# The cast of the output weight to its high part, from ScalarE to VectorE, for weight sets 2 to 11

## The chip, the cores and the metric

The kernel runs on one core of a Trainium2 chip. A core has TensorE (PE, matrix products; its weight loads are shown as PEld), VectorE (DVE), ScalarE (ACT), GpSimd (POOL) and SyncE (SP, which issues the transfers). Each works through its own list of instructions in order and waits for the others by semaphores. The metric is the time of one execution on the device in microseconds (us); before the change it is 969.11 us, the median of 3 runs (968.31 to 970.41).

## The reference, cut to what matters

An attention stage gives x (2304 tokens, 512 wide). Two feed-forward stages follow it:

```
g = x @ w_gate;  val = x @ w_val          # 512 -> 1536
y = (g * sigmoid(g) * val) @ w_out        # 1536 -> 512
h = y @ w2_in                             # 512 -> 2048
out = (max(h, 0) + alpha * min(h, 0)) @ w2_out
```

The inputs q, k, v and all weights are float32 in the reference; the kernel is given the weights as 64-bit floats, which is why a weight element arrives as two 32-bit words and has to be put together on the chip.

## The kernel before, in words

**The first feed-forward stage.** The 2304 tokens are cut into 8 blocks of 288 (HB). The hidden width of 1536 is cut into 12 tiles of 128. Tile j needs weight set j: g (gate), v (value) and o (output), each held as a high part and a low part, so that three products of fp32r stand for one exact product (mm3, L500 to L502: hi by hi, hi by lo, lo by hi). For block and tile PE runs m_g (12 products into g), m_v (12 into v) and, one tile later, m_y (12 into y), 133 ns each at full clock. Between them DVE makes u from g (L544, after a tanh on ACT, L543) and from u and v (L551), ACT casts u to its high part ph (L558) and POOL subtracts to get the low part pl (L559).

**The weights are prepared in the first block only.** For set j the function prep1_ calls w_split for g, v and o in this order, one tile ahead of use. w_split is a chain over three engines: ACT reads the high words with scaling (L129) and the top bytes of the low words (L137); DVE merges the two in place (L139); ACT casts the merged tile st to the high part w[:, 0] (L142); POOL subtracts to get the low part w[:, 1] (L143). For the sets 10 and 11 a shorter buffer is used and DVE merges in two steps, L131 and L132, without L137. st_tile counts its calls in stc[0]: after the o of set j the count is 3(j + 1).

**What else runs in the first block.** The attention of the units from 8 on is prepared beside it: transposes, sums and softmax steps on DVE (L302 to L482), subtractions and sums on POOL (L347, L348, L396, L433, L487), transfers of kn, qn and vd on SP. From the second block on the weights lie ready and only the block's own work and the attention units remain.

**The order.** In this part the order of each engine's list is not written by hand: a scheduler places the instructions by its own estimate of when each can run. So an edit of one instruction moves others on all engines. The names st_1435 and so on below are the merge buffers; st_1340, st_1435, st_1500 belong to the o of the sets 7, 8 and 9, and plain st is the buffer of the sets 10 and 11.

Of the kernel before, what the change touches and what calls it, by code (L numbers as in the profile page):

```python
# [23 lines left out]
def attn_moe_moe2_kernel(  # L24
# [13 lines left out]
    nc = tc.nc  # L38
# [44 lines left out]
    def f32(t):  # L83
        return t.bitcast(F32)
# [26 lines left out]
    stc = [0, None]  # L111

    def top_byte(t):
        return t.rearrange("p f t -> p (f t)").bitcast(U8).rearrange("p (f b) -> p f b", b=8)[:, :, 3]

    def st_tile():
        c = stc[0]
        stc[0] += 1
        if c >= 3 * NEARLY:
            return stp[0].tile([128, 512], F32, tag="st", name="st", bufs=stn[0]), None  # L120
        t = wp.tile([128, 2, 512], F32, tag=st_slots[c % len(st_slots)], name="st2")
        return t[:, 0], t[:, 1]

    def w_split(slot, eng):
        t = raw.pop(slot)
        st, sk = st_tile()
        sti = st.bitcast(I32)
        hw, lw = t[:, :, 1], t[:, :, 0]
        nc.scalar.activation(out=st, in_=hw.bitcast(F32), func=AF.Prelu, scale=2.0 ** -112, alpha=-2.0 ** 32)  # L129
        if sk is None:  # L130
            nc.vector.tensor_scalar(out=sti, in0=sti, scalar1=3, scalar2=None, op0=ALU.logical_shift_left)  # L131
            nc.vector.scalar_tensor_tensor(out=sti, in0=lw, scalar=29, in1=sti,  # L132
                                           op0=ALU.logical_shift_right, op1=ALU.bitwise_or)
        else:

            ski = sk.bitcast(I32)
            nc.scalar.activation(out=ski, in_=top_byte(t), func=AF.Copy,  # L137
                                 scale=1.0 / 32, bias=-31.0 / 64)
            nc.vector.scalar_tensor_tensor(out=sti, in0=sti, scalar=3, in1=ski,  # L139
                                           op0=ALU.logical_shift_left, op1=ALU.bitwise_or)  # L140
        w = W[slot] = wp.tile([128, 2, 512], F32R, tag=slot, name="w")
        nc.scalar.copy(out=w[:, 0], in_=st)  # L142
        eng.tensor_sub(w[:, 1], st, f32(w[:, 0]))  # L143


# [385 lines left out]
    def prep1_(j):  # L531
        for kind in "gvo":
            w_split(f"{kind}{j}", nc.vector if kind in ("", "o", "go", "gvo")[K["lo1"]] else nc.gpsimd)
# [1028 lines left out]
```

## Time and profile before

| what | us |
|---|---|
| median of 3 runs | 969.11 |
| the profiled execution, its own time | 969.31 |
| its span from the first to the last instruction | 967.5 |
| PE busy in the span | 929.8 (96%) |
| DVE busy | 613.2 (63%) |
| ACT busy | 422.7 (44%) |
| POOL busy | 374.2 (39%) |

The shares are means over very different stages. The kernel is full on PE from 135 us on; the change lies in the stretch from 59 to 133 us, where the weights are prepared, and has to be read there.

### The profile page before, as it was taken

To read this page: it belongs to the slowest core of one execution; us is meant where nothing else is said; L and a number is where in the kernel's file an instruction comes from. 1 tells how busy PE (TensorE), PEld (TensorE's weight loads), DVE (VectorE), ACT (ScalarE), POOL (GpSimd) and SP (SyncE) were. 2 spreads that over 40 slices of the span, in tenths; PEclk is the share of its full clock that TensorE was granted. 3 is DMA by queue.
4 is the path that set the end of the run, shared out by engine and by line. 5 is a ranking of instruction groups with operands and counts; after the bars stand their busy time and mean duration, and the time that the engine had idled before them with its cause. 6 is when DMAs were issued, how large, how long until landed. Compare 5 with 4: busy or idle time off the path is not lost.

```text
span 967.5 us, 21670 instructions
## 1 busy us (share of the span) xinstructions
PE 929.8 (96%) x8648; PEld 891.9 (92%) x8648; DVE 613.2 (63%) x1193; ACT 422.7 (44%) x965; POOL 374.2 (39%) x492
## 2 busy tenths in 40 slices
PE   5589889999999999999999998999999999999998
PEld 4479789999999999999999998999999988999998
DVE  5887774546454554535442365777777998777675
ACT  4598732222222132222322356564435774544443
POOL 6389873234422244222222278956251920000000
PEclk9789999999999999999999999999999999999999
DMA  7899641223211141111101346234426882444331
GB/s 190 247 336 373 170 113 34 37 64 59 48 46 24 35 91 34 32 44 22 48 9 53 100 138 212 102 122 149 171 99 231 282 279 87 146 164 150 110 109 44
DMA packets 162091, 116.29 MB, mean 120 GB/s; under 512 B 98889, under 2 KB 143177, under 8 KB 161225
## 3 DMA queue, kind: packets, MB, share of 16 engines
q1 hardware_dynamic: 161927, 114.92, 39.0%
q8 instruction: 67, 1.10, 0.5%
q14 instruction: 33, 0.27, 0.1%
q10 hardware_dynamic: 64, 0.01, 0.0%
HBM read 86.58 MB, written 34.60 MB: 125 GB/s over the span
## 4 chain that ended last, share of the span: by engine, by line
PE 84%; DMA 4%; DVE 3%; POOL 3%; issue 2%; ACT 2%; SPq 1%; DVEq 0%; POOLq 0%; ACTq 0%
PE y L500 5%; PE v L501 5%; PE v L500 5%; PE g L500 4%; PE y L502 4%; PE v L502 4%; PE g L501 4%; PE y L501 4%; PE g L502 4%; PE y L1010 3%; PE y L1011 3%; PE y L1012 3%; PE c L1010 3%; PE c L1011 3%; PE c L1012 3%; PE y L1211 3%
## 5 line engine op out<-in xcount | busy, mean ns | idle before, releaser
L544 DVE SCALAR_TENSOR_TENSOR u<-u,g 128x288 f32<-128x288 f32 x90 | 40.7, 452 | 141.9 <-ACT u L543 141.7
L500 PE MATMUL g<-xh,w 128*128 128x288 f32 x360 | 108.2, 301 | 10.5 <-DVE u L544 4.7
L500 PE MATMUL v<-xh,w 128*128 128x288 f32 x360 | 109.5, 304 | 0.0
L501 PE MATMUL v<-xl,w 128*128 128x288 f32 x360 | 108.9, 302 | 0.0
L502 PE MATMUL g<-xh,w 128*128 128x288 f32 x360 | 107.3, 298 | 0.8 <-POOL w L143 0.8
L502 PE MATMUL v<-xh,w 128*128 128x288 f32 x360 | 107.2, 298 | 0.3 <-POOL w L143 0.3
L501 PE MATMUL g<-xl,w 128*128 128x288 f32 x360 | 107.3, 298 | 0.0
L501 PE MATMUL y<-pl,w 128*128 128x288 f32 x336 | 99.4, 298 | 0.2 <-POOL pl L559 0.2
L502 PE MATMUL y<-ph,w 128*128 128x288 f32 x336 | 99.0, 297 | 0.0
L500 PE MATMUL y<-ph,w 128*128 128x288 f32 x336 | 97.8, 302 | 0.0
L559 POOL TENSOR_TENSOR pl<-u,ph 128x288 fp32r<-128x288 f32 x84 | 70.7, 841 | 57.0 <-ACT ph L558 56.7
L1160 DVE TENSOR_TENSOR hs<-hr,hs 128x512 fp32r<-128x512 f32 x98 | 65.0, 689 | 38.2 <-ACT hs L1154 36.6
L543 ACT ACTIVATE u<-g 128x288 f32<-128x288 f32 x90 | 36.9, 410 | 115.4 <-PE g L502 109.3
L500 PEld LDWEIGHTS g<-xh,w 128*128 128x128 f32 x360 | 68.5, 190 | 12.4 <-DVE u L544 5.4
L558 ACT CAST ph<-u 128x288 fp32r<-128x288 f32 x84 | 36.3, 432 | 89.7 <-DVE u L551 89.7
L501 PEld LDWEIGHTS v<-xl,w 128*128 128x128 f32 x360 | 69.0, 192 | 1.7
L500 PEld LDWEIGHTS v<-xh,w 128*128 128x128 f32 x360 | 68.9, 191 | 1.0 <-DVE u L551 0.5
L502 PEld LDWEIGHTS g<-xh,w 128*128 128x128 f32 x360 | 68.8, 191 | 1.0 <-POOL w L143 1.0
L502 PEld LDWEIGHTS v<-xh,w 128*128 128x128 f32 x360 | 69.0, 192 | 0.5 <-POOL w L143 0.5
L501 PEld LDWEIGHTS g<-xl,w 128*128 128x128 f32 x360 | 68.6, 191 | 0.0
L1154 ACT CAST hs<-hr 128x512 fp32r<-128x512 f32 x98 | 56.9, 622 | 20.6 <-DVE hr L1167 18.8
L500 PEld LDWEIGHTS y<-ph,w 128*128 128x128 f32 x336 | 61.8, 188 | 4.4 <-issue 4.4
(293 smaller groups left out, 2958.7 us busy)
## 6 DMA issues: line engine op xcount, KB each, us to landing
hbuf<-t SPq DMA_DIRECT2D x64, 288.0 KB
hr<-hbuf SPq DMA_DIRECT2D x36, 512.0 KB
raw<-in_moe_w_out_dram SPq DMA_DIRECT2D x28, 512.0 KB
raw<-in_moe_w_in_dram SPq DMA_DIRECT2D x16, 512.0 KB
raw<-in_moe_w_gate_dram SPq DMA_DIRECT2D x12, 512.0 KB
raw<-in_moe_w_val_dram SPq DMA_DIRECT2D x12, 512.0 KB
vw<-vwin SPq DMA_DIRECT2D x48, 96.0 KB
sy<-y SPq DMA_DIRECT2D x8, 576.0 KB
```

Of the source, the lines that this page charges most:

```text
L500: nc.tensor.matmul(o, lhi, rhi, start=first, stop=False)
L501: nc.tensor.matmul(o, lhi, rlo, start=False, stop=False)
L502: nc.tensor.matmul(o, llo, rhi, start=False, stop=last)
L543: nc.scalar.activation(out=u, in_=G[:, :HB], func=AF.Tanh, scale=0.5)
L544: nc.vector.scalar_tensor_tensor(out=u, in0=u, scalar=1.0, in1=G[:, :HB], op0=ALU.add, op1=ALU.mult)
L558: nc.scalar.copy(out=ph, in_=u)
L559: nc.gpsimd.tensor_sub(pl, u, f32(ph))
L1010: nc.tensor.matmul(o, whi[:, ks], yhi[k], start=first, stop=False, skip_group_check=True)
L1011: nc.tensor.matmul(o, whi[:, ks], ylo[k], start=False, stop=False, skip_group_check=True)
L1012: nc.tensor.matmul(o, wlo[:, ks], yhi[k], start=False, stop=k == 1, skip_group_check=True)
L1154: nc.scalar.copy(out=t[:, 0], in_=R[b][SRC[m]])
L1160: vec[0].tensor_sub(t[:, 1], R[b][SRC[m]], f32(t[:, 0]))
```

## The change

In w_split the cast of the merged tile to the high part is given to DVE for the slots whose name begins with o, from the count 7 on, that is for the o of the sets 2 to 11 (10 casts of 128x512). The casts of g and v, and of o of the sets 0 and 1, stay on ACT.

```
         w = W[slot] = wp.tile([128, 2, 512], F32R, tag=slot, name="w")
-        nc.scalar.copy(out=w[:, 0], in_=st)
+        if slot[0] in "o" and stc[0] > 6:
+            nc.vector.tensor_copy(w[:, 0], st)
+        else:
+            nc.scalar.copy(out=w[:, 0], in_=st)
         eng.tensor_sub(w[:, 1], st, f32(w[:, 0]))
```

Lines behind it move down by 3 (L544 becomes L547, L302 becomes L305, and so on).

The first place is DVE's list where the o of the sets 8 and 9 are merged (106 to 116 us in the trace), before:

```order
L139 SCALAR_TENSOR_TENSOR st_1493<-st_1493 128x512
L302 STREAM_TRANSPOSE kT<-kn 128x576
L303 STREAM_TRANSPOSE qT<-qn 128x288
L139 SCALAR_TENSOR_TENSOR st_1435<-st_1435 128x512
L327 TENSOR_REDUCE kd<-kT 128x144
L334 TENSOR_REDUCE qd<-qT 128x72
L139 SCALAR_TENSOR_TENSOR st_1486<-st_1486 128x512
L544 SCALAR_TENSOR_TENSOR u<-u,g 128x288
L131 TENSOR_SCALAR st<-st 128x512
L551 SCALAR_TENSOR_TENSOR u<-u,v 128x288
```

The same place in DVE's list of the changed kernel:

```order
L139 SCALAR_TENSOR_TENSOR st_1435<-st_1435 128x512
L143 CAST w<-st_1435 128x512
L305 STREAM_TRANSPOSE kT<-kn 128x576
L139 SCALAR_TENSOR_TENSOR st_1493<-st_1493 128x512
L306 STREAM_TRANSPOSE qT<-qn 128x288
L330 TENSOR_REDUCE kd<-kT 128x144
L139 SCALAR_TENSOR_TENSOR st_1486<-st_1486 128x512
L337 TENSOR_REDUCE qd<-qT 128x72
L547 SCALAR_TENSOR_TENSOR u<-u,g 128x288
L139 SCALAR_TENSOR_TENSOR st_1500<-st_1500 128x512
L554 SCALAR_TENSOR_TENSOR u<-u,v 128x288
```

The cast of o8 now stands ahead of the transposes and of both u of the tile, and the merge of o9 (st_1500), which stood five rows behind the second u, has moved in front of it.

The second place is the end of the preparation in DVE's list, the merges of the sets 10 and 11 (119 to 132 us), before:

```order
L551 SCALAR_TENSOR_TENSOR u<-u,v 128x288
L426 RECIPROCAL sr_81<-sr_81 128x8
L131 TENSOR_SCALAR st<-st 128x512
L439 TENSOR_TENSOR sm<-sm,sr_81 72x2x144
L131 TENSOR_SCALAR st<-st 128x512
L132 SCALAR_TENSOR_TENSOR st<-raw,st 128x512
L444 STREAM_TRANSPOSE bd_80<-sm 32x6x32 x4
L302 STREAM_TRANSPOSE kT<-kn 128x576
L132 SCALAR_TENSOR_TENSOR st<-raw,st 128x512
L544 SCALAR_TENSOR_TENSOR u<-u,g 128x288
```

And in the changed kernel:

```order
L554 SCALAR_TENSOR_TENSOR u<-u,v 128x288
L131 TENSOR_SCALAR st<-st 128x512
L428 TENSOR_SCALAR sr_81<-sr_81 128x8
L132 SCALAR_TENSOR_TENSOR st<-raw,st 128x512
L429 RECIPROCAL sr_81<-sr_81 128x8
L131 TENSOR_SCALAR st<-st 128x512
L143 CAST w<-st 128x512
L442 TENSOR_TENSOR sm<-sm,sr_81 72x2x144
L132 SCALAR_TENSOR_TENSOR st<-raw,st 128x512
L547 SCALAR_TENSOR_TENSOR u<-u,g 128x288
```

The cast of o10 stands in front of the merge of the next set and of the u that PE needs next; the four transposes L444 have moved behind that u.

## Rows read from the trace of the kernel before

**Rows 1.** Stretches: start:end, length, busy time and instructions of each engine, clock, DMA.

```profile
core 0: us, PE busy (x) PEld busy (x) DVE busy (x) ACT busy (x) POOL busy (x), PEclk, DMA share, GB/s
60.00:98.00 38.00, 35.75 (x336) 34.08 (x335) 29.30 (x50) 32.44 (x74) 33.39 (x30) 0.94 1.02 365
98.34:101.75 3.41, 3.41 (x15) 3.22 (x14) 1.52 (x3) 3.41 (x7) 2.28 (x2) 0.50 0.41 67
110.00:135.00 25.00, 19.41 (x179) 17.20 (x179) 23.19 (x47) 13.73 (x28) 21.24 (x23) 1.00 0.62 141
135.00:250.00 115.00, 115.00 (x1229) 110.12 (x1233) 60.51 (x158) 29.98 (x80) 43.02 (x78) 1.00 0.26 56
250.00:968.00 718.00, 711.62 (x6241) 690.99 (x6240) 448.82 (x822) 299.77 (x662) 230.82 (x275) 1.00 0.34 107
```

**Rows 2.** Waits of PE from 60 to 300 us: total, times, longest.

```profile
PE g L500 <- DVE u L544: 3.3, 2, 2.3
PE g L500 <- ACT w L142: 1.6, 1, 1.6
PE g L500 <- DVE st L131: 1.1, 1, 1.1
PE g L502 <- POOL w L143: 0.8, 1, 0.8
PE att L374 <- DVE qd L334: 0.6, 1, 0.6
PE v L502 <- POOL w L143: 0.3, 1, 0.3
PE y L501 <- POOL pl L559: 0.2, 1, 0.2
```

**Rows 3.** DVE in order of time, the only idle marks from 111 to 134 us.

```profile
111.47 0.69 DVE L139 SCALAR_TENSOR_TENSOR st<-st 128x512 int32<-128x512 int32 x1 [0.86 <-ACT st L137]
...
133.16 0.46 DVE L551 SCALAR_TENSOR_TENSOR u<-u,v 128x288 f32<-128x288 f32 x1 [0.78 <-PE v L502]
```

**Rows 4.** Groups by line: busy us, mean ns, idle before; then shortest/median/longest ns.

```profile
L131 DVE TENSOR_SCALAR st<-st 128x512 int32<-128x512 int32 x6 | 4.5, 750 | 0.0
L131 DVE TENSOR_SCALAR st<-st x6: 404/418/1524, 94.4 to 129.2; 128x512 int32<-128x512 int32 x6
L139 DVE SCALAR_TENSOR_TENSOR st<-st x30: 636/768/1686, 37.2 to 115.3; 128x512 int32<-128x512 int32 x30
L142 ACT CAST w<-st x36: 601/620/636, 40.8 to 132.1; 128x512 fp32r<-128x512 f32 x36
L143 POOL TENSOR_TENSOR w<-st,w x36: 1267/1288/2076, 41.5 to 132.8; 128x512 fp32r<-128x512 f32 x36
L559 POOL TENSOR_TENSOR pl<-u,ph 128x288 fp32r<-128x288 f32 x84 | 70.7, 841 | 57.0 <-ACT ph L558 56.7
```

**Rows 5.** DVE, then POOL, in order of time, 94 to 98 us.

```profile
94.36 1.52 DVE L131 TENSOR_SCALAR st<-st 128x512 int32<-128x512 int32 x1
95.92 1.63 DVE L132 SCALAR_TENSOR_TENSOR st<-raw,st 128x512 int32<-128x512 int32 x1
97.47 0.44 DVE L544 SCALAR_TENSOR_TENSOR u<-u,g 128x288 f32<-128x288 f32 x1
...
94.08 2.92 POOL L143 TENSOR_TENSOR w<-st,w 128x512 fp32r<-128x512 f32 x2 [0.20 <-ACT w L142]
```

**Rows 6.** DVE, then POOL, in order of time, 120 to 123 us.

```profile
120.96 0.41 DVE L131 TENSOR_SCALAR st<-st 128x512 int32<-128x512 int32 x1
121.29 0.67 DVE L132 SCALAR_TENSOR_TENSOR st<-raw,st 128x512 int32<-128x512 int32 x1
...
120.68 1.96 POOL L559 TENSOR_TENSOR pl<-u,ph 128x288 fp32r<-128x288 f32 x1
```

**Rows 7.** All engines' waits from 60 to 140 us: total, times, longest.

```profile
POOL w L143 <- ACT w L142: 7.7, 10, 1.7
ACT st L129 <- DMA raw<-in_moe_w_out_dram: 0.9, 1, 0.9
```

## The prediction, as it was put on record

> **What bounds the kernel now.** I read the stretches first. From 135 us on PE is busy without a gap (115.00 of 115.00 us, then 711.62 of 718) [rows 1]: there the product itself is the bound, so whatever time the first block gains or loses goes through to the end one for one. The edit touches only the first block, so the question is when PE leaves it. Between 60 and 98 us PE lacks 2.25 us (35.75 of 38.00), and between 110 and 135 us 5.6 us (19.41 of 25.00) [rows 1].
>
> Second, what PE waits for in that block. The waits add up to 7.9 us [rows 2]. The longest, 2.3 us, is for the u of L544 at 97.47 us, which stood in DVE's list behind two long merges [rows 2, 5]. All others lie from 110 us on. There PE waits for DVE itself (the second u of 1.0, a sum of 0.6, a merge of 1.1) or for ACT and POOL (1.6, 0.8, 0.3, 0.2), and ACT and POOL are fed by DVE's merges [rows 2].
>
> Third, which engine has no slack there. From 110 to 135 us DVE is busy 23.19 of 25.00 us, POOL 21.24, ACT only 13.73 [rows 1]. In order of time DVE shows two idle marks, 0.86 us before 111.47 and 0.78 us before 133.16, and none in between [rows 3]. So in these 22 us DVE's list is the bound: a microsecond put into it ahead of a u on which PE waits moves the end of the block by a microsecond. Between 60 and 98 us it is otherwise: ACT is busy 32.44 of 38.00 (85%), POOL 88%, DVE 77% [rows 1], and PE is nearly full.
>
> **The change part by part.**
>
> Taken away: ten casts of 0.62 us from ACT [rows 4], 6.2 us of ACT time. Five (o2 to o6) belong to merges ahead of the wait at 97 us, where ACT is loaded; o7 comes just behind it; four (o8 to o11) fall for the most part into the stretch from 110 us on, where ACT has 11 us of idle time [rows 1], and there taking them away gives nothing by itself.
>
> Added: ten casts of 128x512 on DVE. The trace has no such cast on DVE. The nearest row is L131, which also reads one 128x512 tile of 32-bit words in SBUF and writes one: shortest 0.404 us, median 0.418, longest 1.524, mean 0.750 [rows 4]. The length depends on POOL. At 94.36 us L131 ran beside two POOL subtractions and took 1.52 us [rows 5]; at 120.96 us it took 0.41, but then POOL's L559 took 1.96 us instead of its mean of 0.841 [rows 4, 6]. So one of the two waits for the other. With POOL 85% busy (21.24 of 25.00) the undisturbed 0.40 is the lower end for the cast and 1.52 the upper. I take the mean, 0.75, because the six L131 stand in the same lists beside the same subtractions. If the cast ran like the merge L139, its shortest, 0.636, would be the price [rows 4], which lies between.
>
> What the trace cannot tell is whether a cast from f32 to fp32r behaves as L131 does. The Trainium skill, "SBUF — State Buffer", section "Who interferes with whom", says that copies and casts on VectorE can enter a mode that holds a port pair shared with GpSimd, and that whichever comes second is blocked for the whole instruction. By that rule the sum below stands; were the cast free of it, four casts at 0.40 and no burden on POOL would make the sum 1.9 us. That the rule holds for L131 agrees with its 1.52 us beside POOL [rows 5]; for the cast no run here has shown it.
>
> Sum for 105 to 133 us. The casts of o8, o9, o10 and o11 all stand ahead of a u that PE waits for; the order shows o8 and o10 in front of the transposes and of the u. Four casts by 0.75 us are 3.0 us on DVE's list. The merge of o9 also moves ahead of a second u, and four transposes move behind one; both change which wait is late, not the length of the list, so I put them at nothing. Their cover is that the whole list has to be done before PE is free of it; if it fails, the u waits one merge longer, 0.64 to 1.69 us [rows 4]. In turn each cast can hold POOL up by its own 0.40 us; four of them at 85% are 1.4 us, of which PE feels the part of its waits that POOL ends (0.8 + 0.3 + 0.2 of 5.6 us, a quarter) [rows 2]: 0.4 us. POOL's subtraction for o no longer goes over ACT, which would shorten its waits for the cast (7.7 us in ten waits from 60 to 140 us [rows 7]); but the next subtraction is then waiting for the next merge, which DVE brings later, so I count no gain.
>
> Sum for 59 to 105 us. Five casts by 0.75 plus the one of o7 are 4.5 us in 45 us in which DVE has about a quarter idle: covered, except that a u may stand behind a cast. For ACT, 3.7 us less work may bring merges and subtractions earlier and shorten the wait of 2.25 us for the u of 97.47. After that wait the clock was granted at 0.50 from 98.34 to 101.75 us [rows 1], that is 1.2 instead of 2.4 GHz, which cost about half of 3.41, 1.7 us. But PE waits again from 110 us on for DVE's list, so time won at 98 us is mostly waited away there. I take +0.3 us, with -2.25 - 1.7 = -4.0 as the end on the side of a gain and +1.5 (one held cast in front of a u) on the other.
>
> SP's list changes only in order: a gate or value load changes places with transfers of kn, qn and vd between 97 and 130 us. Transfers fill 62% of their engines from 110 us on [rows 1], and ACT waits for a weight there only 0.9 us at one place [rows 7]. I put it at nothing; without that cover it would be that wait again, 0.9 us.
>
> Together 3.0 + 0.4 + 0.3 = **+3.7 us**. The profiled execution took 969.31 us (span 967.5, 1.8 around it), 0.2 above the median of 969.11. So 973.0 against the profiled run, and **972.8 us** against the median.
>
> **The rivals.**
>
> *The cast hides.* The o chain loses one hop: DVE to POOL instead of DVE to ACT to POOL. If PE's late waits are decided by POOL's subtractions and not by the u, the cast of 0.4 replaces 0.62 plus a hand-over, POOL runs on earlier, and the 1.3 us of PE's waits for POOL [rows 2] go, which pays for most of four undisturbed casts (4 by 0.40 are 1.6). That gives +0.3: 969.4, no measurable difference. For it: POOL waits for the cast ten times [rows 7]. Against it: the largest of PE's waits are for DVE and ACT, not POOL [rows 2]. It decides if POOL's idle time in front of the subtraction, not DVE's list, is what the block ends on.
>
> *Faster through ACT.* With 3.7 us less on ACT ahead of 105 us, the merges at 91 to 97 us come earlier, the u of 97.47 is not held, and the clock is not lowered. Gain up to 2.25 + 1.7 = 4.0 us, 965.1. It decides only if DVE's list from 105 us on also begins earlier by as much and its four casts fit into that lead; DVE's solid list of 22 us [rows 3] speaks against it.
>
> *Held at every turn.* If each of the four casts comes second to a subtraction, it costs 1.52 instead of 0.75, 6.1 us in place of 3.0: 975.8 with the small terms. Against it: the median L131 was not held [rows 4].
>
> That the change does not do what it says is excluded: the order has ten casts on DVE.
>
> **How the numbers follow.** My forecast, +1.3 (four casts at 0.32 past the overlap, nothing else) to +5.5 around +3.7, has a chance of 0.60; held at every turn 0.10; the cast hides 0.22; faster 0.08. A measurement of this kernel tells 0.2% (1.9 us) from no change. The part of the forecast under +1.9 is small and I weigh it against the part of the hiding case above it. So slower 0.71, same 0.21, faster 0.08. The range goes from 969.3, where the hidden case lies, to 975.8, the held case; this leaves out the faster case and the tails.
>
> **What would show it.** In the changed profile DVE should have ten casts of 0.40 us at the shortest and about 0.7 on the mean, some over 1 us, each beside a POOL subtraction; PE's waits from 105 us to the last one of the block should add up to 8 or 9 us instead of 5.6, with those for DVE's u grown; DVE's idle mark of 133.16 [rows 3], the end of its list, should stand at about 137; ACT should stay under 60% there; from 140 us on PE should be full as before. I am wrong if the casts stay at 0.40 and PE's waits do not grow (the cast hides), if the wait at 98 us and the lower clock vanish and the block ends earlier (faster), or if a change in the later blocks appears.

## The result, and the profile after

The changed kernel took 975.65 us (median of 6 runs, 973.22 to 978.18) beside 969.76 us for the kernel before on the same chip: ratio 1.007, 95% interval 1.0054 to 1.0087, so about 6.8 us slower (5.2 to 8.4). The forecast was +3.7 us, 972.8, at most 975.8. The sign was right, the size too small by almost half; the median lies just under the upper end, which belonged to a rival. The profiled execution took 975.53 us (span 973.7).

Stretches of the changed kernel, columns as in [rows 1]:

```profile
60.00:98.00 38.00, 34.12 (x324) 31.89 (x324) 28.95 (x54) 28.48 (x66) 28.93 (x28) 0.96 1.01 356
110.00:135.00 25.00, 18.22 (x164) 16.94 (x164) 24.89 (x45) 12.14 (x25) 18.77 (x21) 0.92 0.54 126
135.00:140.00 5.00, 5.00 (x29) 5.00 (x29) 3.22 (x5) 0.84 (x3) 3.63 (x5) 0.69 0.37 73
140.00:250.00 110.00, 110.00 (x1227) 105.13 (x1226) 60.86 (x159) 29.20 (x78) 40.22 (x74) 1.00 0.27 58
250.00:974.00 724.00, 717.75 (x6288) 696.98 (x6286) 450.56 (x825) 300.93 (x665) 233.66 (x280) 1.00 0.34 106
```

From 140 us on nothing changed: PE lacks 6.25 us behind 250 us, before 6.38 [rows 1]. All of the loss lies in the first block, and not only in its late part: between 60 and 98 us PE now lacks 3.88 us where it lacked 2.25, between 110 and 135 us 6.78 where it lacked 5.59. The clock was granted at 0.50 from 117.6 to 121.0 us and from 134.7 to 138.1 us, behind waits of 2.24 and 2.10 us.

PE's waits from 60 to 300 us (total, times, longest), then waits of ACT, and the same ACT line in the kernel before:

```profile
PE g L503 <- DVE u L547: 5.7, 6, 1.8
PE g L505 <- POOL w L146: 2.8, 2, 2.1
PE att L377 <- DVE qd L337: 2.2, 1, 2.2
PE y L503 <- DVE qs L485: 0.8, 1, 0.8
PE att L373 <- DVE qT L306: 0.5, 1, 0.5
PE v L503 <- DVE u L554: 0.4, 1, 0.4
PE y L504 <- POOL pl L562: 0.3, 1, 0.3
```

```profile
ACT st L129 <- POOL w L146: 4.7, 7, 1.2
```

```profile
ACT st L129 <- POOL w L143: 1.7, 3, 0.9
```

The waits add up to 12.7 us instead of 7.9 [rows 2]. More than half of the growth lies ahead of 105 us, where the forecast allowed 0.3: 4.9 us instead of 2.3. From 105 us on it is 7.7 instead of 5.6; the forecast said 8 or 9. ACT now waits longer for a buffer that POOL's subtraction holds: 4.7 us in seven waits instead of 1.7 in three.

DVE's ten casts from 55 to 140 us (group, then shortest/median/longest), and two rows of DVE in order of time, the second of which is the same u as the one of 133.16 in [rows 3]:

```profile
L143 DVE CAST w<-st 128x512 fp32r<-128x512 f32 x10 | 6.7, 667 | 0.1
L143 DVE CAST w<-st x10: 384/428/1398, 59.0 to 137.9; 128x512 fp32r<-128x512 f32 x10
```

```profile
137.22 0.78 DVE L305 STREAM_TRANSPOSE kT<-kn 128x576 f32<-128x576 f32 x1 [0.73 <-DMA kn<-in_k_dram]
...
141.09 0.45 DVE L554 SCALAR_TENSOR_TENSOR u<-u,v 128x288 f32<-128x288 f32 x1 [0.37 <-PE v L505]
```

The casts cost what was forecast (0.384 shortest, 0.667 mean). The mark did not come out. An idle mark does stand at 137.22, near the forecast 137, but it is a transpose that waits for a transfer; the u that stood at 133.16, the second one of the block's last tile, now stands at 141.09, 7.9 us later. So the casts are as long as was forecast, and still 3 us are missing.

### The profile page after: what moved, and what is told of

It is laid out like the page before. It is cut to its first block, busy times and chain, and to the rows that moved or that the text cites. A ratio compares the mean times of both kernels' runs of the same rounds, so it can differ in the third digit from the quotient of the medians.

```text
span 973.7 us, 21674 instructions
## 1 busy us (share of the span) xinstructions
PE 931.0 (96%) x8648; PEld 892.4 (92%) x8648; DVE 619.9 (64%) x1203; ACT 417.6 (43%) x955; POOL 372.0 (38%) x492
## 4 chain that ended last, share of the span: by engine, by line
PE 82%; SPq 5%; DMA 5%; POOL 3%; DVE 3%; issue 2%; ACT 1%; DVEq 0%; POOLq 0%
PE y L503 5%; PE y L505 4%; PE v L504 4%; PE y L504 4%; PE v L503 4%; PE g L503 4%; PE g L505 4%; PE g L504 4%; PE v L505 4%; PE y L1013 3%; PE y L1014 3%; PE y L1015 3%; PE c L1013 3%; PE c L1014 3%; PE c L1015 3%; PE y L1214 3%
## 5 line engine op out<-in xcount | busy, mean ns | idle before, releaser
L547 DVE SCALAR_TENSOR_TENSOR u<-u,g 128x288 f32<-128x288 f32 x90 | 40.7, 452 | 142.1 <-ACT u L546 142.0
```

Source lines behind the costliest of these rows:

```text
L547: nc.vector.scalar_tensor_tensor(out=u, in0=u, scalar=1.0, in1=G[:, :HB], op0=ALU.add, op1=ALU.mult)
```

## The experiments

Ratios were taken against the kernel before on the same chip; us are the ratio's excess times 969, with the 95% interval. The line numbers of the variants are shifted. "Row order" is the order of an engine's instructions; it is computed by the scheduler from the whole program and changed on all five engines when the casts moved: of the 1056 rows that are held below, 562 stand at another place of their list. Where a run below does not hold the order, its edit moved other rows too; that is said there.

**Order and casts apart.** Each engine's rows of the first block are held in a given order by edges of order only (no waits); the ten casts themselves are left free to stand where the scheduler puts them.

```diff
+PIN = [
...
+]
...
+                rows = {x.name: x for x in nc.cur_bb.bb.instructions}
+                for one in PIN:
+                    one = [f"I-{x}" for x in one.split()]
+                    for x, y in zip(one, one[1:]):
+                        tc.add_manual_dep(rows[y], x, mybir.DependencyInfo(
+                            mybir.DependencyClass.NoSync, mybir.DependencyReason.DATA), reason="pin")
```

The order of after with the casts on ACT (the kernel before plus that list):

> Every engine's list is held in the row order of the changed kernel, but the ten casts are back on ACT. So it has the reordering without the casts. Theory 1 (the prediction's: the casts' own time on DVE's list is the price, the order costs nothing): 0 to +1 us against before, PE's waits from 60 us on 7 to 9 us as before (7.8). Theory 2 (the price is the order that came with the casts: merges of o drawn forward ahead of a u, late clock window): +3 us or more, with waits ahead of 105 us of about 4.9 us as in the changed kernel and not 2.25.

Measured +4.7 us (3.3 to 6.2). Its PE waits:

```profile
PE g L509 <- DVE u L553: 6.3, 7, 1.5
PE g L511 <- POOL w L152: 3.3, 2, 2.2
PE g L509 <- ACT w L151: 1.1, 2, 0.8
PE y L509 <- DVE qs L491: 0.9, 1, 0.9
```

With 0.6 and 0.5 us of two further lines they sum to 12.7 us, as in the changed kernel. These lie ahead of 105 us, 5.1 us together, as theory 2 forecast:

```profile
PE g L509 <- DVE u L553: 3.6, 4, 1.3
PE y L509 <- DVE qs L491: 0.9, 1, 0.9
PE y L510 <- POOL pl L568: 0.6, 2, 0.3
```

So the new order costs something with not one cast on DVE. It is not the price of the order in the changed kernel, though: the order was computed for casts on DVE, and with the casts on ACT POOL waits 12.5 us for them instead of 7.7 [rows 7].

The order of before with the casts on DVE (the changed kernel plus the other list), then the same with the casts of six or of four sets:

> Every engine's list is held in the row order of the kernel before, and the ten casts stand on DVE, each directly behind its merge. So it has the casts without the reordering. Theory 1: +3.7 to +6.8 us against before, PE's waits from 105 us on 8 to 9 us instead of 5.6. Theory 2: 0 to +3 us. If both theories hold a part, this run and the one with the casts on ACT add up to about the +6.8 us of the change.

> The order of the kernel before, with only the casts of the first six sets (o2 to o7) on DVE, those of o8 to o11 on ACT. Theory 1 as on record: +0.3 us (bounds -4.0 to +1.5), since DVE has a quarter of its time idle between 60 and 98 us. Rival: an early cast in front of a u holds that u and PE has no later wait that gives it back: +2 to +4 us, with new PE waits for u between 60 and 100 us of 0.4 to 1.5 us each.

> The order of the kernel before, with only the casts of o8 to o11 on DVE, o2 to o7 on ACT. Theory 1 as on record: +3.4 us (four casts of 0.75 us on a full list plus 0.4 by POOL; bounds 1.3 to 6.1), all of it as longer PE waits between 105 and 135 us. Theory 2 (order) and the rival that the cast hides behind POOL: 0 to +1 us.

```diff
-        if slot[0] in "o" and stc[0] > 6:
+        if slot[0] in "o" and 6 < stc[0] <= 24:
```

```diff
-        if slot[0] in "o" and stc[0] > 6:
+        if slot[0] in "o" and stc[0] > 24:
```

Measured +5.8 us (4.1 to 7.6) for all ten, +1.6 (0.6 to 2.6) for the first six, +5.3 (3.4 to 7.3) for the last four. The first of these met theory 1 and not theory 2. So either part alone costs nearly as much as the whole, and they do not add: 4.7 + 5.8 is more than 6.8. And four casts that take 2.0 us in sum (mean 0.49) cost 5.3. This is the riddle on which the later runs work. One part of the expectation was untrue: the casts did not stand directly behind their merges, but 2, 3, 2, 1, 1, 1, 3, 4, 8 and 1 rows behind (in the changed kernel 2, 1, 2, 3, 1, 1, 1, 5, 3 and 3).

The traces, one execution each, split these times by stretch. The last column is the start of the last row u<-u,v of the trace, in the eighth block, against 588.88 us in the kernel before.

| run | all runs, us | PE's waits 60 to 105 us | from 105 us | last u later by |
|---|---|---|---|---|
| kernel before | | 2.3 | 5.6 | |
| changed kernel | +6.8 | 4.9 | 7.7 | 6.08 |
| order of after, casts on ACT | +4.7 | 5.1 | 7.6 | 3.95 |
| order of before, ten casts on DVE | +5.8 | 3.5 | 7.6 | 6.08 |
| order of before, first six | +1.6 | 3.7 | 5.2 | 0.55 |
| order of before, last four | +5.3 | 2.2 | 7.3 | 2.41 |

```profile
588.88 0.46 DVE L551 SCALAR_TENSOR_TENSOR u<-u,v 128x288 f32<-128x288 f32 x1
```

```profile
591.29 0.46 DVE L563 SCALAR_TENSOR_TENSOR u<-u,v 128x288 f32<-128x288 f32 x1
```

The two rows are the kernel before and the run with the last four casts. Of that run's loss, half had come by then. The rest came behind it, where the program is the same: from 601.7 to 608.5 us the clock was granted at 0.50 (last section), which the kernel before does not show. The run with the first six has such a stretch from 599.2 to 606.0 us. By these two traces such a stretch is worth about 2 us (an estimate: from the last u to the end they take 381.0 and 380.6 us, the kernel before 378.6). So a difference of that size between two runs can come from a place that the edit does not touch, and the small prices, 1.6 above all, hang on it. The order held by edges costs little by itself, since the run with the first six holds it too.

**PE's clock.** Filler matmuls in three of PE's waits of the changed kernel:

```diff
+            if blk == 0 and e == 3 and j in FILL:
+                for _ in range(FILL[j][1]):
+                    more.append(nc.tensor.matmul(Y[0][0:64, 0, 0:128], ident[0:64, 64:128], ident[0:64, :],
+                                                 start=False, stop=False).ins)
```

> The changed kernel in its own row order, with 17 extra matmuls that add zeros to an open sum (64x128, lhs a zero block of the identity): 7 ahead of the matmul that waits at 116.32, 4 ahead of the one at 125.43, 6 inside the wait at 133.16. At 0.21 us each they fill about 70% of those three waits and delay nothing that is ready. Theory A (a part of the 6.8 us that the prediction left out is PE's clock: granted 0.50 from 117.6 to 121.0 and from 134.7 to 138.1 us, behind the waits): the two low stretches go, the late one is worth 1.7 us at the end, so 1.5 to 2.0 us less than the changed kernel, +4.6 to +5.1 us against before. Theory B (DVE's list alone carries the cost, the clock is waited away): the same as the changed kernel, +6.6 us, within 0.5.

Measured +6.8 us (4.7 to 8.9). The two low stretches did go; the stretch from 112 us, PE's longest group of waits, and two groups of DVE from 132 to 140 us, followed by the same two in the changed kernel from 131 to 139.4:

```profile
112.00:140.00 28.00, 21.51 (x202) 19.41 (x201) 27.89 (x47) 11.09 (x23) 20.19 (x23) 1.00 0.52 121
```

```profile
PE g L514 <- DVE u L558: 8.2, 8, 2.1
```

```profile
L142 DVE TENSOR_SCALAR st<-st 128x512 int32<-128x512 int32 x2 | 2.9, 1436 | 0.0
L143 DVE SCALAR_TENSOR_TENSOR st<-raw,st 128x512 int32<-128x512 int32 x2 | 2.7, 1362 | 0.0
```

```profile
L132 DVE SCALAR_TENSOR_TENSOR st<-raw,st 128x512 int32<-128x512 int32 x2 | 1.8, 891 | 0.0
L131 DVE TENSOR_SCALAR st<-st 128x512 int32<-128x512 int32 x2 | 1.3, 656 | 0.0
```

The clock was granted at 1.00 all through, PE waited longer for u (8.2 us instead of 5.7); the two steps of the last two merges took 5.6 us instead of 3.1. The measured time is theory B's, and the trace speaks for it, but the interval still holds theory A's 4.6 to 5.1: that the clock is no part of the missing term is likely and not shown.

**Where a u stands.** Four first u's of the kernel before, six of the changed one, moved up in DVE's list (one of the six as an example: the u is row 1231, behind four transposes of which the first was running):

```diff
-1199 891 892 893 894 1231 1244
+1199 891 1231 892 893 894 1244
```

> The kernel before in its own row order but for four first u's on DVE: each that stood behind something longer (97.47 behind a merge, 118.55 behind a sum pair, 125.26 behind transposes and two merges, 131.93 behind a merge) is put directly behind the instruction that ran when its tanh was done. DVE's list has the same work. Theory A (where a u stands in the list decides, not the length of the list): -1.5 to -3 us against before, the wait of 2.25 us at 97.97 gone. Theory B (the length of the list between 105 and 133 us decides): -0.5 to +0.5 us, the time that is won at 98 us is waited away later, in waits for weights instead of u.

> The changed kernel in its own row order but for six first u's on DVE (67.02, 80.93, 86.81, 116.19, 124.94, 129.55), each put directly behind the instruction that ran when its tanh was done, ahead of casts, merges, sums and transposes that stood in front of it. Same work. Theory A: the early loss of about 2.2 us (u's behind a merge and a cast at 67, 81 and 87 us) goes, and 1 to 2 us of the late one: +3 to +4.5 us against before instead of +6.6. Theory B: the list's length holds the end, at most the early part changes and is waited away: +6 to +7 us.

Measured +2.1 us (0.9 to 3.4) and +6.0 (3.9 to 8.0). In the kernel before theory A falls, and theory B's -0.5 to +0.5 was missed as well; its trace has the last u at 589.00 us, 0.1 later than before, and a low clock from 599.2 to 606.0 us behind it. There PE's waits for u fell from 3.3 to 1.6 us, and those for a weight that ACT casts rose from 1.6 to 2.8: what a u gained, a weight lost. In the changed kernel the waits for u fell from 5.7 to 3.6 and the time stayed; the interval does not exclude theory A's +3 to +4.5.

**Less work on DVE.** Two reliefs at once, on either kernel, then one of them alone:

```diff
-        if c >= 3 * NEARLY:
+        if c >= 3 * NEARLY + 3:
```

```diff
-        d["act"] = K["a1" if n < 2 * NP else "a2"]
+        d["act"] = K["a1" if n <= 2 * NP else "a2"]
...
-        dn = n < 2 * NP and K["dnP"]
+        dn = n <= 2 * NP and K["dnP"]
```

> The kernel before (casts on ACT) with less on DVE's late list: the three splits of set 10 merge with ACT's help (one pass of ACT and L139 in place of L131 and L132, 0.596 + 1.063 - 1.160 = 0.50 us less on DVE each), and the ninth attention unit subtracts and sums in ACT's exponential and divides on ACT (0.44 + 0.41 + 0.76 us less, about 0.1 more on DVE). Together 3.0 us off the list between 105 and 133 us. If DVE's list bounds that stretch: -3.0 us against before (-1.0 to -5.6, all that PE waits there). If POOL or the transfers bound it beside DVE: 0 to -0.5 us.

> The changed kernel with the same relief of DVE's late list by 3.0 us. If the list bounds the stretch in both: +3.6 us against before (+6.6 - 3.0). If most of the change's cost is the order and POOL's hold-up, not the length of DVE's list: still +5.5 us or more.

> The kernel before, only the ninth attention unit's softmax moved from DVE to ACT (the subtraction, the sum and the division of its 72x288 part: 0.44 + 0.41 + 0.76 us off DVE between 110 and 125 us, a 72x4 scale of about 0.1 us on). The other half of the earlier relief, the merges of set 10, is left as it was. If the length of DVE's list in that stretch sets the end: -1.5 us against before. If the loss of 12 us in the earlier run came from this half, +3 us or more; if it came from the merges' buffers, this run has none of it. If not DVE's list but the subtractions on POOL bound the stretch: 0.

> The changed kernel with the same move of the ninth unit's softmax to ACT, 1.5 us off DVE's list. If the length of DVE's list sets the end: +5.1 us against before instead of +6.6. If the casts' cost lies in the order or in POOL: +6 to +7 us.

Measured +11.9 us (9.6 to 14.1) and +16.1 (13.8 to 18.5) with both; +0.6 (-0.7 to +1.8) and +7.1 (5.6 to 8.6) with the second alone. The first two came out far slower than any of their forecasts would have it; the last two came out where DVE's list is not the bound (0, and +6 to +7). None of the four holds the order. The waits of the first, from 105 to 140 us:

```profile
PE g L500 <- ACT w L142: 5.0, 1, 5.0
...
ACT w L142 <- POOL w L143: 2.4, 2, 1.6
...
ACT st L129 <- DVE st L132: 2.1, 1, 2.1
```

The merges of set 10 now use the buffers of weights that are still to come, so ACT's cast waits for POOL, and PE 5.0 us for a cast: less work, but a buffer that comes free later (argued from these waits, and the order moved too). The other two say less than they were to say, for the list did not get 1.5 us shorter. The scale that took the place of the subtraction was priced at 0.1 us and took 1.0 in the kernel before and 1.3 in the changed one, from 105 to 140 us:

```profile
L391 DVE TENSOR_SCALAR nb<-mx 72x4 f32<-72x4 f32 x1 | 1.0, 1025 | 0.0
```

```profile
L394 DVE TENSOR_SCALAR nb<-mx 72x4 f32<-72x4 f32 x1 | 1.3, 1309 | 0.0
```

From 105 to 135 us DVE is busy 26.93 us instead of 27.84 in the first and 28.20 instead of 28.29 in the second. Whether a shorter list ends earlier was not tested by them.

**POOL and DVE together.** The cast in another form, in the changed kernel and in the order of before; and POOL's value sums moved to DVE:

```diff
-            nc.vector.tensor_copy(w[:, 0], st)
+            nc.vector.tensor_copy(w[:, 0].rearrange("p (a b) -> p b a", b=2), st.rearrange("p (a b) -> p b a", b=2))
```

```diff
-            nc.vector.tensor_copy(w[:, 0], st)
+            nc.vector.tensor_reduce(out=w[:, 0], in_=st.unsqueeze(2), axis=AX.X, op=ALU.max)
```

```diff
             for f in range(2):
-                if n < NP:
+                if n < 3 * NP:
                     nc.vector.reduce_sum(vs[:, f], hu[n]["vd"][f].rearrange("p h (r c) -> p h c r", r=4), axis=AX.X)
```

> The changed kernel in its own row order, the ten casts on DVE read and write every second element (two passes of 256), so the same cast in a slower form. If the spread of the casts in the changed kernel (0.38 to 1.40 us) is an exclusion between DVE's fast form and POOL, the strided casts are all nearly equal (0.55 to 0.75 us, spread under 0.1) whatever POOL does. If it is ordinary contention in SBUF, they spread as before, up to 1.4 us or more. The sum of ten is 5.5 to 7.5 us against 6.7, so the time stays within 1 us of the changed kernel by either.

> The changed kernel in its own row order, the ten casts on DVE done as a reduce over one element (128x512 to 128x512, high part). By the rows of the reduces (72x288 0.448 us, 128x576 0.736, never longer) one takes about 0.67 us, as much as the mean of the ten casts (0.667), so DVE's list is as long as in the changed kernel; but a reduce is not held by POOL and does not hold it. Theory P (POOL and DVE's merges and casts exclude each other, that pair is full): ten times about 0.4 us leave the pair, 2 to 4 us less than the changed kernel, +2.6 to +4.6 us against before. Theory L (the length of DVE's list): +6.6 us as the changed kernel.

> The row order of the kernel before with the ten casts on DVE as reduces (beside the earlier run with plain casts in that order, +5.8 us). Theory P: 2 to 4 us less than that, +1.8 to +3.8 us against before. Theory L: +5.8 us.

> The kernel before with the value sums of attention units nine to twelve (POOL, 6 x 0.84 and 5 x 0.70 us between 105 and 140 us) as reduces of 72x512 on DVE, about 0.67 us each, some 4 us more on DVE's list there and 8 us less on POOL. Theory P: the pair is relieved by up to 8 us, -1.5 to -5 us against before. Theory L: +3 to +5 us.

> The changed kernel with the same sums on DVE. Theory P: +1.5 to +5 us against before instead of +6.6. Theory L: +9.5 to +11.5 us.

Measured +5.9 us (3.9 to 7.8) with the strided cast; +5.4 (3.5 to 7.4) and +6.9 (5.2 to 8.4) with the reduces; +2.9 (1.5 to 4.3) and +6.2 (4.6 to 7.8) with the sums. One and the same cast, that of o4, and the POOL operation beside it, in order of time: in the changed kernel, strided, as a reduce.

```profile
73.67 1.40 DVE L143 CAST w<-st 128x512 fp32r<-128x512 f32 x1
...
73.48 1.30 POOL L146 TENSOR_TENSOR w<-st,w 128x512 fp32r<-128x512 f32 x1 [2.43 <-ACT w L145]
```

```profile
71.89 1.43 DVE L152 CAST w<-st 128x512 fp32r<-128x512 f32 x1
...
71.69 1.30 POOL L155 TENSOR_TENSOR w<-st,w 128x512 fp32r<-128x512 f32 x1 [1.24 <-ACT w L154]
```

```profile
72.12 0.68 DVE L152 TENSOR_REDUCE w<-st 128x512 fp32r<-128x512 f32 x1
...
71.94 1.31 POOL L155 TENSOR_TENSOR w<-st,w 128x512 fp32r<-128x512 f32 x1 [1.86 <-ACT w L154]
```

```profile
L152 DVE TENSOR_REDUCE w<-st x10: 644/678/686, 58.2 to 135.3; 128x512 fp32r<-128x512 f32 x10
```

The exclusion is real: a cast that begins beside the subtraction ends 0.29 us (73.67 + 1.40 - 74.78) or 0.33 us behind it, strided or not, and the reduce is not held at all. But taking the casts out of it saves nothing that these intervals can show, in the order of before least of all (6.9, where theory P said 1.8 to 3.8; in the changed kernel the interval reaches into its 2.6 to 4.6). The sums on DVE slowed the kernel before by 2.9 where the full pair of DVE and POOL forecast a gain; those two runs do not hold the order. As the explanation of the size theory P is not borne out, and not excluded: in the single traces the reduces bring the last u to 592.02 and 592.65 us, where plain casts in the same orders have 594.96 in both. Theory L holds for the sums in the kernel before, and for those in the changed one neither forecast was met.

**The place of the cast.** In the run with the last four on DVE (+5.3), DVE from 121 us, then POOL and ACT:

```profile
121.44 0.68 DVE L141 SCALAR_TENSOR_TENSOR st<-raw,st 128x512 int32<-128x512 int32 x1
122.04 1.51 DVE L456 STREAM_TRANSPOSE bd<-sm 32x192 f32<-32x192 f32 x4
...
125.22 0.41 DVE L152 CAST w<-st 128x512 fp32r<-128x512 f32 x1
...
127.71 0.43 DVE L140 TENSOR_SCALAR st<-st 128x512 int32<-128x512 int32 x1 [1.41 <-ACT st L138]
...
125.71 1.27 POOL L155 TENSOR_TENSOR w<-st,w 128x512 fp32r<-128x512 f32 x1 [2.94 <-DVE w L152]
...
127.01 0.66 ACT L138 ACTIVATE st<-raw 128x512 f32<-128x512 f32 x1 [1.77 <-POOL w L155]
```

The merge of o10 was done at 122.12. Its cast came 3.1 us later, behind transposes, a merge and a u; POOL idled 2.94 us for it, ACT 1.77 us for the buffer that POOL held, DVE 1.41 us for ACT. It is a ring: merge, cast, subtraction, buffer, next merge. On ACT, which is half idle there, the same cast began in the kernel before 0.1 us behind its merge [rows 6]:

```profile
122.06 0.62 ACT L142 CAST w<-st 128x512 fp32r<-128x512 f32 x1 [0.69 <-DVE st L132]
```

Two runs put the cast into the row behind its merge, else the same order (in DVE's list; 1618 and 1725 are merges, 1620 and 1727 the casts of o10 and o11, which the earlier list left free):

```diff
-1710 1618 1692 1693
+1710 1618 1620 1692 1693
...
-2156 1725 1793 1806
+2156 1725 1727 1793 1806
```

> The order of the kernel before, the casts of o8 to o11 on DVE, each in the row directly behind its merge; in the earlier run with these four (+5.3 us) they stood 3, 4, 8 and 1 rows behind it. The same work on every engine. Theory C (the price is the late place of the cast: POOL's subtraction, the release of the buffer and the next merge wait for it in a ring): +1.5 to +2.5 us against before, what four casts of 0.4 to 0.6 us take of DVE's list. Theory L (list length, wherever the cast stands): +5.3 us.

> The order of the kernel before, all ten casts on DVE, nine of them in the row directly behind the merge, the first one row later; in the earlier run (+5.8 us) they stood 2, 3, 2, 1, 1, 1, 3, 4, 8 and 1 rows behind it. Theory C: +2 to +4 us against before. Theory L: +5.8 us.

Measured +2.2 us (1.2 to 3.3) instead of 5.3 for the last four, and +5.1 (3.8 to 6.5) instead of 5.8 for all ten. The four casts and the one of o10 with its subtraction:

```profile
L152 DVE CAST w<-st 128x512 fp32r<-128x512 f32 x4 | 2.9, 736 | 0.1
```

```profile
121.08 0.92 DVE L152 CAST w<-st 128x512 fp32r<-128x512 f32 x1
...
122.08 1.29 POOL L155 TENSOR_TENSOR w<-st,w 128x512 fp32r<-128x512 f32 x1 [0.36 <-DVE w L152]
```

For the late four theory C holds: the casts even took longer (2.9 us against 2.0, held by POOL), POOL's wait ahead of that subtraction shrank from 2.94 to 0.36, and 3.1 us came back. In the two traces 2.65 us are there at the last u, 588.64 us instead of 591.29; what is lost behind it goes with the low clock. For all ten it is not seen: 5.1 is hardly less than 5.8, and above theory C's 2 to 4. By difference the early six cost 5.1 - 2.2 = 2.9 us directly behind their merges, not less than the 1.6 of the run in which they stood up to three rows later; as such prices do not add, this is an estimate.

## Why the size was wrong

- **The bound and the direction: right.** PE is full from 140 us on, and the loss goes through: the last u stands 6.1 us later, the end of the profiled execution 6.2. The end of DVE's list was forecast about 4 us later and came 7.9 later (133.16 to 141.09).
- **Four casts of 0.75 and 0.4 for POOL, 3.4 us: the length was right, the place was left out.** In the changed kernel the late four took 2.4 us (0.92, 0.41, 0.73 and 0.38), less than the 3.0 of the sum. In the old order they cost 2.2 us (1.2 to 3.3) directly behind their merges, for 2.9 us on the list, and 5.3 (3.4 to 7.3) where they were left free, for 2.0.
- **The order, put at nothing: the step that failed.** The prediction said of the moved merges and transposes that "both change which wait is late, not the length of the list, so I put them at nothing", and put SP's order at nothing too. The order of after with the casts on ACT costs 4.7 us (3.3 to 6.2), and PE's waits ahead of 105 us are 5.1 us there, as long as in the changed kernel (4.9; before 2.3). The moved rows thus cost time in the very stretch for which the sum had +0.3. Moved rows add nothing to the list's length; that only the length counts was wrong. The same four casts in the same order of all other rows cost 3.1 us more where they stand 3, 4, 8 and 1 rows behind their merges, though they take less time there. What share of the changed kernel's 6.8 us is the order's stays open: with the casts on DVE the old order has 5.8 or 5.1, so that the new one adds only 1.0 to 1.7, within the noise.
- **The subtraction "no longer goes over ACT ... I count no gain": it can be a loss.** The hop to ACT went through an engine with idle time; on DVE the cast queues behind whatever stands there, and the buffer stays held. The trace of the late four shows it for o10 (2.94 us of POOL, 1.77 of ACT). ACT's waits for buffers that POOL holds grew from 1.7 to 4.7 us, but not by the casts alone: they are 3.4 us in the order of after with the casts on ACT, and 2.0 with ten casts on DVE directly behind their merges.
- **Stretch 59 to 105 us, +0.3: too small for the changed kernel.** PE waits 2.6 us longer there, 2.8 longer in the same order with the casts on ACT, and 1.2 longer with the casts on DVE in the old order, so most of it goes with the order. For the casts alone the term is not refuted: six early casts cost 1.6 us in the old order (interval 0.6 to 2.6, the forecast's upper bound was 1.5), of which 0.55 are there at the last u, and by difference 2.9 when they stand directly behind their merges.
- **What the parts make together.** Late four 2.2, early six 1.6 to 2.9, order 4.7: the sum is 8.5 to 9.8, measured were 6.8. They share waits, so none can be subtracted cleanly; the order that the scheduler makes fits casts on DVE (1.0 over the old order) better than casts on ACT (4.7), but is not shown to be better than the old order with casts placed by hand (5.1, interval 3.8 to 6.5, against 6.8, 5.2 to 8.4).
- **The rivals.** "Held at every turn" gave the right time, 975.8, by luck: of the late four it wanted all held and 6.1 us, and two were held and all four took 2.4; a cast that can't be held costs about as much. The cast did not hide, and the gain through ACT did not come: the wait at 97 us went, but others came ahead of it (67.52, 76.97, 81.42 us and later).
- **The Trainium skill.** The exclusion that the prediction took from "SBUF — State Buffer", section "Who interferes with whom", holds for this cast (1.40 us beside POOL, 0.43 alone), and so does its remark that on trn2 a reduce never contends (0.644 to 0.686 us). The strided form was my own guess; "VectorE: DVE Perf Modes", section "Mode 2×_2P — use both read ports for one tensor", asks for operands in SBUF and an even outermost dimension, and names no stride. Both held for the strided cast, and its 1.43 us beside POOL and 0.41 at the shortest agree.

What stays open is which rows of the new order cost the 4.7 us. The rows show the places (first u's behind a merge at 66 and 80 us, a subtraction at 131), but moving the u's changed nothing that the interval shows, and no run takes one engine's order back alone. Open too are the share of the order in the 6.8 us, whether a shorter list on DVE would end earlier, and why the low clock behind 599 us comes in some executions. No run was faster than the kernel before.

## What to carry to other kernels

Where a scheduler computes the order, a moved instruction has two prices, its time and the reordering, and the second can be as large: hold the row order by edges and run all four combinations before pricing the rest. Price a moved step by who waits for it: follow its output to the buffer that it keeps held and back to the next producer, and look at how many rows it stands behind its input. A relief is one only if the trace shows the list shorter. And before a small difference is given to an edit, look in the trace whether it is already there where the edit ends.

## What the runs showed of the hardware

- The exclusion of POOL and DVE reaches plain and strided casts alike, and can be longer than one operation: the merge at 128.42 us of the run with four late casts took 2.58 us beside two POOL operations in a row (128.41 to 130.44 us); the merge at 124.28 took 0.65 us.

```profile
128.42 2.58 DVE L141 SCALAR_TENSOR_TENSOR st<-raw,st 128x512 int32<-128x512 int32 x1
```

- PE's clock differs between executions at places where the code is the same. The first row is the kernel before, the two others the run with the last four casts on DVE: there the grant was 0.50 from 601.7 to 608.5 us, though PE had waited no longer between 595 and 605 us (2.7 and 2.6 of 10 us). Eleven of the eighteen variants' traces have such a stretch between 599 and 624 us. Executions of the kernel before alone list mean grants from 0.981 to 0.998 and spread over 4 to 7 us on one chip, so a few tenths of a per cent need several runs of both kernels on one chip.

```profile
595.00:605.00 10.00, 7.27 (x49) 6.39 (x48) 5.47 (x9) 7.93 (x19) 6.50 (x7) 1.00 0.59 189
```

```profile
595.00:605.00 10.00, 7.39 (x44) 6.58 (x43) 6.27 (x10) 6.21 (x16) 7.78 (x7) 0.83 0.66 222
...
601.70:608.50 6.80, 5.73 (x24) 5.37 (x24) 3.40 (x4) 4.18 (x11) 3.43 (x3) 0.50 0.28 89
```
